# Strassen's identity in the down projection of a linear-attention and feed-forward kernel

## The chip, the cores and the metric

The kernel runs on one core of one Trainium2 chip. A core has five engines that run side by side, each with an instruction queue of its own that it works off in order: TensorE (PE in the profile, with its weight loads as PEld), VectorE (DVE), ScalarE (ACT), GpSimd (POOL) and SyncE (SP), which here only issues DMA transfers. They hand work to each other by semaphores. Matmuls write into PSUM, which has 8 banks of 512 four-byte columns in each of 128 partitions. The metric is device time in microseconds (us); lower is better.

## What is computed

Two stages follow each other. The first is attention with a decaying state over 4 sequences of 768 positions and 8 heads of 64; the second is a feed-forward layer, which takes the attention's output as 3,072 tokens of 512 features:

```python
h = x @ w_in                          # (3072, 512) @ (512, 2048)
g = h * (1.0 / (1.0 + np.exp(-h)))    # SiLU
return (g @ w_out).astype(np.float32) # (3072, 2048) @ (2048, 512)
```

Inputs and the output are float32; the kernel multiplies in bf16 and sums in float32.

## The kernel before, in words

**Groups.** The tokens are handled in 12 groups of 256, numbered g = 0 to 11 in the code (the change's "groups 3 to 12" are g = 2 to 11). A group is two chunks of 128 tokens, 24 chunks in all. The attention of a pair of chunks is a "section" of small 64 by 64 matmuls (`section`, the matmuls at line 540). A section can do three things at once: the outputs of one pair of chunks (tile `op`), and the scores (`sp`) and the states (`kv_ps`) of the next pair. Behind its matmuls it puts on VectorE and ScalarE: the copies of the outputs into `xt` (one half of the features on each engine), then on VectorE two masked score copies `ss` (line 560) and for each state an addition to the running `total` (line 570 or 572) and a cast of it to `kvs`.

**Up projection.** `ffn1_two(g, i)`, i = 0 to 7, does 8 matmuls of 256 columns (line 604) into one PSUM bank with the tag "h", and ScalarE then applies SiLU to the whole bank (line 609) and writes a bf16 tile `g` of 2 by 256 columns. There are two "h" banks, so the unit i+2 can't start before the SiLU of unit i has read its bank.

**Down projection.** `downs(g)` gives 8 units of `ffn2`: for each of the two token halves `mt`, four units of 4 matmuls of 512 columns (line 642), which is 32 matmuls per group. Each half fills one bank of tags "o0" and "o1", which take turns, and VectorE copies it to SBUF (line 648), from where SP stores it: outputs of the first six groups wait in the list `held` until no more input loads are to come, later ones go to `stores` and are issued two units later. The last half of the last group is cut in three (`ffn2_last`, line 662), so that its last copy and store are small.

**Order.** The order of the instructions on each engine is the order of the Python calls; nothing reorders them. In the loop at line 807 a group is: 8 up units, then 8 down units. Before the third down unit (i = 2) come the input scaling on GpSimd (`preps`), transposes by DMA and the loads of later chunks; before the second and the fourth come the casts of `v` on ScalarE (`vcast`); before the seventh (i = 6, line 836) comes the section. So when the next group's up projection starts, two down units lie between it and the section. In g = 3 a second section stands before up unit 7 (line 818), and in g = 2 before down unit 1 (line 822). Sections of g = 3 to 9 compute scores and states too; those before i = 6 of g = 2 and g = 10 only outputs.

**PSUM.** The 8 banks are o0, o1, two "h", three "att" and one "kv". The section borrows the free one of o0 and o1 for one score bank (`other()`), and both "h" banks for its outputs.

**Waits.** Dependences between engines are found by the layer that records the program, from the parts of the tiles that instructions read and write.

## Time and profile before

| | us |
|---|---|
| three runs | 206.22, 205.32, 206.63 |
| median of them | 206.22 |
| span of the profiled execution, first to last instruction | 203.8 |
| TensorE busy in it | 196.6 (96%) |
| VectorE busy | 81.5 (40%) |
| ScalarE busy | 90.0 (44%) |
| GpSimd busy | 53.5 (26%) |

The profiled execution's span is 2.4 us under the median of the runs. Busy TensorE time counts each matmul to its modelled end, so that matmuls overlap in it; how fast they really follow each other is read from the chain of waits, where 64 of them or 24 of them stand as one piece with its length. In the profile's rows "out<-in" are tiles, 128x512 the partitions and elements of the tile written, "x368" a count, and then come the total busy time and the mean of one in ns. The granted clock of TensorE is 1.00 in most of the span; it is 0.99 as a mean.

### The profile page before, as it was taken

The numbers are of one execution on the slowest core, as the hardware profiler recorded it, in microseconds if no ns is written. First come the engines' busy times: TensorE is split into PE (matmuls) and PEld (weight loads), VectorE is DVE, ScalarE is ACT, GpSimd is POOL, SyncE is SP. The second block draws the span as 40 slices with busy tenths as digits, with TensorE's granted clock in tenths as the row PEclk, the third lists the DMA queues.
The fourth block names the chain that finished last, engine by engine and source line by source line (L and its number), as shares of the span: only waits on it lengthen the run. The fifth ranks groups of instructions, "written<-read, shape, count | busy, mean of one in ns | idle before, by whom it ended". The sixth has DMA issues, their size and how long they took to land.

```text
span 203.8 us, 6077 instructions
## 1 busy us (share of the span) xinstructions
PE 196.6 (96%) x2636; PEld 130.5 (64%) x2636; DVE 81.5 (40%) x176; ACT 90.0 (44%) x165; POOL 53.5 (26%) x98
## 2 busy tenths in 40 slices
PE   7689999999999899999999999999999999999994
PEld 2368444557747656856856856856856856856854
DVE  1897357294072085515315415414315415412011
ACT  3864973454704731641641641741741741622610
POOL 5240002657062126434425153440400000000000
PEclk9969999999999999999999999999999999999999
DMA  4999999999679949849789594997997601101102
GB/s 107 336 369 408 400 408 270 279 266 211 148 151 164 239 80 246 194 83 227 162 187 201 116 264 91 226 215 169 269 384 152 245 2 55 53 3 55 51 2 103
DMA packets 95579, 38.67 MB, mean 190 GB/s; under 512 B 80960, under 2 KB 88512, under 8 KB 95552
## 3 DMA queue, kind: packets, MB, share of 16 engines
q1 hardware_dynamic: 91248, 37.24, 70.5%
q10 hardware_dynamic: 4304, 1.05, 3.1%
q8 instruction: 20, 0.33, 0.7%
q14 instruction: 7, 0.06, 0.1%
HBM read 27.27 MB, written 6.29 MB: 165 GB/s over the span
## 4 chain that ended last, share of the span: by engine, by line
PE 64%; DMA 2%; SPq 1%; ACT 1%; issue 0%; POOL 0%; DVE 0%
PE o_ps L642 29%; PE h_ps L604 28%; PE op L540 3%; DMA vf<-in_v_dram 2%; PE o_part L662 2%; PE sp L540 1%; SPq L391 1%; PE kv_ps L540 1%; ACT vb L178 0%; POOL kb L364 0%; ACT g L609 0%; DVE ob L182 0%; SPq L390 0%
## 5 line engine op out<-in xcount | busy, mean ns | idle before, releaser
L642 PE MATMUL o_ps<-w_out_bf,g 128*128 128x512 bf16 x368 | 83.8, 379 | 0.0
L604 PE MATMUL h_ps<-xt,w_in_bf 128*128 128x256 bf16 x672 | 75.7, 273 | 1.0 <-ACT g L609 1.0
L604 PEld LDWEIGHTS <-w_in_bf 128*128 128x128 bf16 x672 | 65.6, 98 | 11.2 <-issue 1.1
L609 ACT ACTIVATE g<-h_ps 128x512 bf16<-128x512 f32 x84 | 49.9, 597 | 41.3 <-PE h_ps L604 41.0
L642 PEld LDWEIGHTS <-g 128*128 128x128 bf16 x368 | 34.8, 98 | 38.3
L178 ACT ACTIVATE xt<-op 128x256 bf16<-128x256 f32 (+1 forms) x18 | 8.3, 487 | 46.9 <-issue 34.4
L364 POOL TENSOR_TENSOR qb<-qf,lam_fwd 128x256 bf16<-128x256 f32 x18 | 11.3, 625 | 59.7 <-issue 31.3
L648 DVE COPY ob<-o_ps 128x512 f32<-128x512 f32 x11 | 7.6, 689 | 46.6 <-PE o_ps L642 46.6
L560 DVE TENSOR_TENSOR ss<-sp,mask 128x512 bf16<-128x512 f32 x20 | 12.8, 682 | 14.9 <-PE sp L540 14.9
L182 DVE CAST xt<-op 128x256 bf16<-128x256 f32 (+1 forms) x16 | 8.3, 543 | 21.2 <-PE op L540 20.1
L648 DVE COPY pair<-o_ps 128x512 f32<-128x512 f32 x12 | 8.2, 686 | 16.5 <-PE o_ps L642 16.5
L572 DVE TENSOR_TENSOR total<-total,kv_ps 128x256 f32<-128x256 f32 x33 | 13.6, 414 | 0.1
L364 POOL TENSOR_TENSOR kb<-kf,lam_bwd 128x256 bf16<-128x256 f32 x20 | 12.4, 618 | 4.6 <-DMA kf<-in_k_dram 3.4
L365 POOL TENSOR_TENSOR kb<-kf,lam_bwd 128x256 bf16<-128x256 f32 x20 | 12.5, 625 | 0.0
L178 ACT ACTIVATE vb<-vf 128x512 bf16<-128x512 f32 x20 | 11.6, 622 | 0.9 <-DMA vf<-in_v_dram 0.9
L365 POOL TENSOR_TENSOR qb<-qf,lam_fwd 128x256 bf16<-128x256 f32 x18 | 11.2, 620 | 0.0
L182 DVE CAST kvs<-total 128x256 bf16<-128x256 f32 x33 | 10.5, 319 | 1.1
L698 PE MATMUL h_ps<-xt,w_in_bf 128*128 128x512 bf16 x48 | 10.5, 379 | 0.0
L540 PEld LDWEIGHTS <-vb 64*64 64x64 bf16 x320 | 7.5, 105 | 4.5 <-issue 4.2
L540 PE MATMUL op<-ss,vb 64*64 64x64 bf16 x320 | 9.9, 199 | 0.0
L540 PE MATMUL op<-qt,kvs 64*64 64x64 bf16 x296 | 9.6, 194 | 0.0
L698 PEld LDWEIGHTS <-w_in_bf 128*128 128x128 bf16 x48 | 4.7, 98 | 5.4
(76 smaller groups left out, 126.2 us busy)
## 6 DMA issues: line engine op xcount, KB each, us to landing
kf<-in_k_dram SPq DMA_DIRECT2D x19, 256.0 KB, 4.5
vf<-in_v_dram SPq DMA_DIRECT2D x18, 256.0 KB, 4.2
qf<-in_q_dram SPq DMA_DIRECT2D x17, 256.0 KB, 4.0
pair<-in_moe_w_out_dram SPq DMA_DIRECT2D x8, 512.0 KB, 7.8
pair<-in_moe_w_in_dram SPq DMA_DIRECT2D x6, 512.0 KB, 7.3
out_dram<-pair SPq DMA_DIRECT2D x12, 256.0 KB, 3.9
out_dram<-ob SPq DMA_DIRECT2D x11, 256.0 KB, 3.8
pair<-in_k_dram SPq DMA_DIRECT2D x4, 256.0 KB, 4.5
```

The lines of the kernel that those rows point to most:

```text
L178: nc.scalar.activation(dst, src, AF.Copy)
L182: nc.vector.tensor_copy(dst, src)
L364: eng.tensor_tensor(dst[:, 0::2], src[:, 0::2, ::-1, :], by[:, 0::2, ::-1, :], op=AL.mult)
L365: eng.tensor_tensor(dst[:, 1::2], src[:, 1::2], by[:, 1::2], op=AL.mult)
L540: ins = nc.tensor.matmul(dst, lhsT=lhsT, rhs=rhs, start=start, stop=True, skip_group_check=True)
L560: nc.vector.tensor_tensor(ss, sp.rearrange("k w p q -> k (w p) q"), mask64[:, None, :].to_broadcast([128, len(scores) * NP, D]), op=AL.mult)
L572: nc.vector.tensor_tensor(total[b], old, place(c, h), op=AL.add)
L604: nc.tensor.matmul(hps[g, i][:, a:a + 256], lhsT=w_in_bf[:, ko, m * 128:(m + 1) * 128], rhs=xt[g][:, ko, :], start=(ko == 0 and u == 0), s ...
L609: nc.scalar.activation(gg.rearrange("p u n -> p (u n)"), hps[g, i], AF.Silu)
L642: nc.tensor.matmul(o, lhsT=gt[g, ko][:, mt * BLK:(mt + 1) * BLK], rhs=w_out_bf[:, ko, :], start=(ko == 0), stop=(ko == KO_OUT - 1))
L648: nc.vector.tensor_copy(ob, o)
L698: nc.tensor.matmul(hps["m", m], lhsT=w_in_bf[:, ko, m * 128:(m + 1) * 128], rhs=xall[0][:, :, ko, :], start=(ko == 0), stop=(ko == KO_IN - 1))
```

## The change

The down projection of g = 2 to 11 is a product of a 256 by 2048 matrix (the group's `g`, stored transposed) with the 2048 by 512 matrix `w_out`. The change cuts both into 2 by 2 blocks of 128 tokens, 1024 inner positions (8 matmuls, `K2`) and 256 output columns (`HALF`), and replaces the eight block products by Strassen's seven. Each product is 8 matmuls of 256 columns, 56 per group. Groups 0 and 1 stay as they were.

What it needs beside the products:

- `weight_sum`: the five sums and differences of blocks of `w_out` that the identity uses, once, in ten VectorE additions of 128x1024 bf16 elements. Four come before g = 2, six between its first up units.
- `g_sums(g, i)`, after each up unit: for i < 4 one VectorE subtraction of 128x256 bf16 elements (`gd`), for i > 3 an addition of 128x256 (`gc`), one of 128x512 (`gb`) and a subtraction of 128x256 (`gd`). Operands and results are bf16 in SBUF.
- Recombination in place of the two copies: `after_4`, `after_6`, `after_2` and `after_7`, with float32 operands in PSUM and SBUF.

```diff
-        for i, unit in enumerate(downs(g)):
+            ups(g, i)                              # ffn1_two, then g_sums
+            if g == 2 and i < 6:
+                weight_sum(*sums[4 + i])
+        for i, unit in enumerate(seven(g)):
...
-            if i == 6:
+            if i == 5:
...
-                section((c, d), cs, steps(*cs) if cs else (), "AD", many[:2] if cs else many, other())
+                section((c, d), cs, steps(*cs) if cs else (), "AD", many[:2] if cs else many)
```

The products and what follows each (`seven`; o[0] and o[1] are the banks o0 and o1, each with two places of 256 columns):

```python
def product(g, n, dst, start):
    tick()
    for k in range(K2):
        if n in (3, 4):
            lhsT = gt[g, k][:, 0:128] if n == 3 else gt[g, K2 + k][:, 128:256]
        else:
            lhsT = gs[g, n, k]
        rhs = w_block(n, k, (0, 0))[:, 0, :] if n == 2 else w_block(n, k, (1, 1))[:, 0, :] if n == 5 else wsum[n, k]
        nc.tensor.matmul(dst, lhsT=lhsT, rhs=rhs, start=(start and k == 0), stop=(k == K2 - 1), skip_group_check=True)
...
def after_4():
    nc.scalar.activation(m, o[0][:, 0, :], AF.Copy)
    nc.vector.tensor_tensor(m, m, o[0][:, 1, :], op=AL.add)
def after_6():
    nc.vector.tensor_tensor(m, m, o[1][:, 0, :], op=AL.add)
def after_2():
    nc.vector.tensor_tensor(quarters[:, 0::3, :], m[:, None, :].to_broadcast([128, 2, HALF]), o[0], op=AL.subtract)
    nc.scalar.activation(quarters[:, 1:3, :], o[0], AF.Copy)
    if last:
        put(0, (HALF, DM), quarters[:, 1, :])
        put(1, (0, HALF), quarters[:, 2, :])
        nc.vector.tensor_tensor(quarters[:, 3, :], quarters[:, 3, :], o[1][:, 1, :], op=AL.add)
        put(1, (HALF, DM), quarters[:, 3, :])
def after_7():
    if last:
        nc.vector.tensor_tensor(quarters[:, 0, :], quarters[:, 0, :], tail, op=AL.add)
        put(0, (0, HALF), quarters[:, 0, :])
        return
    nc.vector.tensor_tensor(quarters[:, 0::3, :], quarters[:, 0::3, :], o[1], op=AL.add)
...
order = [(3, 0, 0, True, None), (4, 0, 1, False, after_4), (1, 1, 0, True, None), (6, 1, 1, False, after_6),
         (5, 0, 0, False, None), (2, 0, 1, False, after_2), (7, 1, 0, True, after_7)]
```

`quarters` is the output tile of the group as four pieces of 256 columns: token half 0 in pieces 0 and 1, token half 1 in pieces 2 and 3. Product 2 and product 5 use blocks of `w_out` as they are, products 3 and 4 blocks of `g` as they are. For the last group product 7 goes to an "h" bank (`tail`), and the four pieces are stored one by one (`put` issues the DMA at once); `ffn2_last` goes away.

In the loop, the section now stands before the sixth of seven products (product 2), and no longer borrows an "o" bank; its third bank comes from "att". The ring of output tiles has 2 tiles of 1,024 columns in place of 4 of 512.

More of the change, by code (lines that the diff above doesn't have):

```diff
@@ L67 @@
     gpool = ctx.enter_context(tc.tile_pool(name="gpool", bufs=26))
-    opool = ctx.enter_context(tc.tile_pool(name="opool", bufs=4))
+    opool = ctx.enter_context(tc.tile_pool(name="opool", bufs=2))
     psum = ctx.enter_context(tc.tile_pool(name="psum", bufs=1, space=bass.MemoryType.PSUM))
@@ L611, in ffn1_close @@
             gt[g, 2 * i + u] = gg[:, u, :]
+        gt[g, 2 * i, "pair"] = gg
     def ffn1_two(g, i):
@@ L646, in ffn2 @@
             nout[0] += 1
-            ob = opool.tile([128, DM], F32, name="ob", tag="ob") if n > 11 else pairs[n // 2][:, DM * (n % 2):DM * (n % 2) + DM]
+            ob = pairs[n // 2][:, DM * (n % 2):DM * (n % 2) + DM]
             nc.vector.tensor_copy(ob, o)
             r0 = gstart[g] + mt * BLK
-            dst = out[r0:r0 + BLK, :]
-            if n > 11:
-                stores.append([0, dst, ob])
-            else:
-                held.append((dst, ob))
-    def ffn2_last(g, mt):
-        r0 = gstart[g] + mt * BLK
-        for i, (a, z, tag) in enumerate([(0, 256, "o"), (256, 384, "h"), (384, 512, "h")]):
-            o = psum.tile([128, 512], F32, name="o_part", **bank(tag))
-            for ko in range(KO_OUT):
-                nc.tensor.matmul(o[:, :z - a], lhsT=gt[g, ko][:, mt * BLK:(mt + 1) * BLK], rhs=w_out_bf[:, ko, a:z],
-                                 start=(ko == 0), stop=(ko == KO_OUT - 1))
-            ob = opool.tile([128, DM], F32, name="ob", tag="ob")
-            move("A" if i == 1 else "D", ob[:, :z - a], o[:, :z - a])
-            tick(0)
-            nc.sync.dma_start(out=out[r0:r0 + BLK, a:z], in_=ob[:, :z - a])
+            held.append((out[r0:r0 + BLK, :], ob))
@@ new lines, with w_block, weight_sum @@
+    HALF = DM // 2
+    K2 = KO_OUT // 2
+    wsum = {}
+    WSUMS = (
+        (3, "subtract", (0, 1), (1, 1), "kp"),
+        (4, "subtract", (1, 0), (0, 0), "vp"),
+        (1, "add", (0, 0), (1, 1), "qtp"),
+        (6, "add", (0, 0), (0, 1), "ktp"),
+        (7, "add", (1, 0), (1, 1), "qb2"),
+    )
+    def w_block(n, k, blk, size=1):
+        row, col = blk
+        return w_out_bf[:, K2 * row + k:K2 * row + k + size, HALF * col:HALF * col + HALF]
+    def weight_sum(i, h):
+        n, op, a, b, tag = WSUMS[i]
+        t = nat.tile([128, K2 // 2, HALF], BF16, name=f"wsum{n}", tag=tag, bufs=2)
+        k = K2 // 2 * h
+        nc.vector.tensor_tensor(t, w_block(n, k, a, K2 // 2), w_block(n, k, b, K2 // 2), op=getattr(AL, op))
+        for x in range(K2 // 2):
+            wsum[n, k + x] = t[:, x, :]
@@ new lines, with g_sums @@
+    gs = {}
+    def g_sums(g, i):
+        lo, hi = slice(0, 128), slice(128, 256)
+        one = gt[g, 2 * i, "pair"]
+        first = i < K2 // 2
+        d = gpool.tile([128, 2, 128], BF16, name="gd", tag="g", padded_shape=[128, 2, 256])
+        if not first:
+            low = gt[g, 2 * i - K2, "pair"]
+            cross = gpool.tile([128, 2, 128], BF16, name="gc", tag="g", padded_shape=[128, 2, 256])
+            nc.vector.tensor_tensor(cross, low[:, :, lo], one[:, :, hi], op=AL.add)
+            both = gpool.tile([128, 2, 256], BF16, name="gb", tag="g")
+            nc.vector.tensor_tensor(both, low, one, op=AL.add)
+        a, b = (hi, lo) if first else (lo, hi)
+        nc.vector.tensor_tensor(d, one[:, :, a], one[:, :, b], op=AL.subtract)
+        for u in range(2):
+            k = 2 * i + u - (0 if first else K2)
+            gs[g, 6 if first else 7, k] = d[:, u, :]
+            if not first:
+                gs[g, 1, k] = cross[:, u, :]
+                gs[g, 5, k] = both[:, u, lo]
+                gs[g, 2, k] = both[:, u, hi]
@@ new lines, in product, with seven, put, step @@
+    def product(g, n, dst, start):
+        tick()
+        for k in range(K2):
+            if n in (3, 4):
+                lhsT = gt[g, k][:, 0:128] if n == 3 else gt[g, K2 + k][:, 128:256]
+            else:
+                lhsT = gs[g, n, k]
+            rhs = w_block(n, k, (0, 0))[:, 0, :] if n == 2 else w_block(n, k, (1, 1))[:, 0, :] if n == 5 else wsum[n, k]
+            nc.tensor.matmul(dst, lhsT=lhsT, rhs=rhs, start=(start and k == 0), stop=(k == K2 - 1), skip_group_check=True)
+    def seven(g):
+        o = [psum.tile([128, 2, HALF], F32, name="o_ps", **bank("o")) for _ in range(2)]
+        last = g == len(GROUPS) - 1
+        tail = psum.tile([128, HALF], F32, name="o_tail", tag="h", bufs=2, padded_shape=[128, 512]) if last else None
+        ob = pairs[g] if g < 6 else opool.tile([128, 4 * HALF], F32, name="ob", tag="ob")
+        quarters = ob.rearrange("p (a n) -> p a n", a=4)
+        m = work.tile([128, HALF], F32, name="msum", tag="msum", bufs=2)
+        r0 = gstart[g]
+        def put(rows, cols, src):
+            dst = out[r0 + BLK * rows:r0 + BLK * rows + BLK, cols[0]:cols[1]]
+            if last:
+                nc.sync.dma_start(out=dst, in_=src)
+            elif g < 6:
+                held.append((dst, src))
+            else:
+                stores.append([0, dst, src])
+        def after_4():
[12 more added lines that the diff above has]
+        def after_7():
+            if last:
+                nc.vector.tensor_tensor(quarters[:, 0, :], quarters[:, 0, :], tail, op=AL.add)
+                put(0, (0, HALF), quarters[:, 0, :])
+                return
+            nc.vector.tensor_tensor(quarters[:, 0::3, :], quarters[:, 0::3, :], o[1], op=AL.add)
+            for t in range(2):
+                put(t, (0, DM), ob[:, DM * t:DM * t + DM])
+        order = [(3, 0, 0, True, None), (4, 0, 1, False, after_4), (1, 1, 0, True, None), (6, 1, 1, False, after_6),
+                 (5, 0, 0, False, None), (2, 0, 1, False, after_2), (7, 1, 0, True, after_7)]
+        def step(n, b, x, start, after):
+            def run():
+                product(g, n, tail if n == 7 and last else o[b][:, x, :], start)
+                if after:
+                    after()
+            return run
+        return [step(*x) for x in order]
@@ L794, with ups @@
     down0(3, 1)
-    def downs(g):
-        return [(g, mt, range(4 * kk, 4 * kk + 4)) for mt in range(2) for kk in range(4)]
-    def other():
-        return f"o{1 - otag[0]}", 1
+    sums = [(i, h) for i in range(len(WSUMS)) for h in range(2)]
+    for x in sums[:4]:
+        weight_sum(*x)
     def steps(*cs):
         return [(c, h) for c, h in [(cs[0] - 1, 1)] + [(c, h) for c in cs for h in range(2)] if c > 5][:-1]
+    def ups(g, i):
+        ffn1_two(g, i)
+        g_sums(g, i)
     many = (("h", 2),) * 2 + (("att", 3),) * 2
@@ L819 @@
                 section((), (c, d), steps(c, d))
-            ffn1_two(g, i)
-        for i, unit in enumerate(downs(g)):
+            ups(g, i)
+            if g == 2 and i < 6:
+                weight_sum(*sums[4 + i])
+        for i, unit in enumerate(seven(g)):
             if i == 1 and g == 2:
                 section((), (c, d), steps(c, d))
-            if i == 1 and g > 2:
+            if i == 2 and g > 2:
                 vcast(a)
@@ L835 @@
                 load_vs(10, 11, e=nc.scalar)
-            if i == 6:
+            if i == 5:
                 cs = [x for x in (a, b) if g > 2 and x < NCHUNK]
-                section((c, d), cs, steps(*cs) if cs else (), "AD", many[:2] if cs else many, other())
-            ffn2(*unit)
+                section((c, d), cs, steps(*cs) if cs else (), "AD", many[:2] if cs else many)
+            unit()
     g = len(GROUPS) - 1
     for i in range(8):
-        ffn1_two(g, i)
-    for unit in downs(g)[:4]:
-        ffn2(*unit)
-    ffn2_last(g, 1)
+        ups(g, i)
+    for unit in seven(g):
+        unit()
 _INS = ['q', 'k', 'v', 'lam', 'moe_w_in', 'moe_w_out']
```

## The prediction, made before the changed kernel ran

> **What bounds the kernel now.** I read the page first: which engine is full, and what the chain that ended last is made of.

> ```profile
> PE 196.6 (96%) x2636; PEld 130.5 (64%) x2636; DVE 81.5 (40%) x176; ACT 90.0 (44%) x165; POOL 53.5 (26%) x98
> ...
> PE o_ps L642 29%; PE h_ps L604 28%; PE op L540 3%; DMA vf<-in_v_dram 2%; PE o_part L662 2%; PE sp L540 1%; SPq L391 1%; PE kv_ps L540 1%; ACT vb L178 0%; POOL kb L364 0%; ACT g L609 0%; DVE ob L182 0%; SPq L390 0%
> ```

> TensorE is the path; VectorE has room as a mean. Next the chain in order of time through one group (g = 7), since busy time counts overlapped matmuls twice (start, length, both us).

> ```profile
> 126.45 6.99 PE h_ps L604 x64
> 133.44 5.18 PE o_ps L642 x24
> 138.62 0.15 PE op L540 x2
> ...
> 140.01 1.83 PE o_ps L642 x8
> ```

> A group is 6.99 us of up projection, 7.01 (5.18 + 1.83) of down projection and a section of about 1.4 between its two parts. 64 matmuls of 256 columns take 6.99, so 0.1092 each; 24 of 512 take 5.18, so 0.2158. Cost per column is nearly the same, weight loads (98 ns each in the page's groups) are hidden at either width.

> Third, the timeline of VectorE and, below it, of ScalarE, behind the section that ends at 93.88:

> ```profile
> 94.10 0.69 DVE L182 CAST xt<-op 128x512 bf16<-128x512 f32 x1 [2.37 <-PE op L540]
> 94.70 1.28 DVE L560 TENSOR_TENSOR ss<-sp,mask 128x512 bf16<-128x512 f32 x2
> ...
> 97.66 0.30 DVE L182 CAST kvs<-total 128x256 bf16<-128x256 f32 x1
> 97.87 0.69 DVE L648 COPY pair<-o_ps 128x512 f32<-128x512 f32 x1
> ```

> ```profile
> 96.70 0.60 ACT L609 ACTIVATE g<-h_ps 128x512 bf16<-128x512 f32 x1 [2.12 <-PE h_ps L604]
> 97.57 0.60 ACT L609 ACTIVATE g<-h_ps 128x512 bf16<-128x512 f32 x1 [0.28 <-PE h_ps L604]
> ```

> VectorE works for nearly 4 us behind a section, past the next up projection's start (95.79 in the chain). The copy of the down result comes last, at 97.87, though its bank was full at 95.79. That is harmless now: nobody waits for it. Meanwhile ScalarE does the first SiLU at 96.70.

> **The change, part by part.**

> *Products.* 56 x 0.1092 = 6.12 us in place of 7.01: -0.89 in nine groups; the last has 3.45 + 3.55 = 7.00, so -0.88. Sum -8.9.

> *The copy in after_2.* This decides. VectorE subtracts into pieces 0 and 3 of the output tile, then ScalarE copies pieces 1 and 2. They are disjoint, but the stretch from piece 0 to piece 3 covers 1 and 2. In the built program the ScalarE copy waits for VectorE at the subtraction's count and not for TensorE. The subtraction stands on VectorE behind the whole section; the copy stands on ScalarE ahead of all SiLUs of the next group; the third up unit needs the first SiLU. From the up projection's start T:

> - The subtraction can start when the copy at L648 starts now: D = 3.25, 2.08, 2.77, 2.74, 2.10, 2.72 and 2.71 after T, for the sections of g = 3 to 9 (97.87 - 95.79 = 2.08 is g = 4; the two short ones have three states, the others four). Two products (1.75) lie behind the section where 1.83 lay, so add 0.08.
> - Subtraction 0.68 (row ss, 682 ns, same size, one operand in PSUM), hand-over 0.05, copy 0.60 (row xt<-op on ACT), of which the next ACT instruction waits 0.50 (starts in a back-to-back pair differ by that), SiLU 0.60, hand-over 0.04.
> - The SiLU ends at T + D + 1.95; the third unit wants to start at T + 1.75. Stall: D + 0.20.

> Sum over seven: 18.37 + 1.4 = 19.8 us. With free hand-overs, and ScalarE's next instruction charged nothing beyond the subtraction: D - 0.39, 15.6. Later SiLUs come every 0.50, units every 0.87, so no second stall. In g = 2 and 10 the section leaves only output copies and the subtraction is in time.

> *Small sums.* No bf16 addition from SBUF is in the trace. Nearest rows: a bf16 to bf16 copy of 512 elements takes 424 ns where f32 to bf16 takes 692, so 16-bit data go at the double rate; at that rate 256, 512 and 1024 elements cost 0.21, 0.34 and 0.61 us back to back (the last by the w_out cast, 693 ns). At the single rate (rows total and ss) 0.33, 0.60 and about 1.2. I take the double rate. Per up unit with i > 3 that is 0.76 against 0.87 of TensorE: VectorE keeps up, and product 1, the first to need `gc`, starts two products later. At the single rate the backlog is four times 0.4, and product 1 has 1.5 us of slack: about nothing.

> *Products 5 and 7* wait for after_4 and after_6. after_4 is 0.42 on ACT and 0.41 on DVE while products 1 and 6 (1.75) run: hidden, if VectorE is free. *ScalarE's after_4 copy* delays the two casts of v by 1.3 us; they still end before the section needs them (0.8 left). *Stores and loads on SP* move with their units; SP waits for after_7, with nothing urgent behind. The third "att" bank is drained a group earlier. All nothing.

> *First group (g = 2).* VectorE is not free here. From 48.4 (its last copy) it does 10 x 0.61 + 12 x 0.21 + 4 x 0.34 = 10.0 us, plus collisions: a cast at 83.16 took 0.73 in place of 0.29 while GpSimd worked, 0.44 per collision. Three such are 1.3: 59.7. Then the scores and states of the section put before product 4 (3.2), and after_4 (0.41): 63.3. Product 5 would start at 54.6 + 4 x 0.874 + 0.65 = 58.8, so 4.5 lost; of it 1.0 returns, since g = 3 now waits 1.0 for ScalarE (longest wait of TensorE on `g`), held by a DMA. Net +3.5. Bounds: no collision +2.2, all eleven GpSimd operations there +7.0, single rate +12. [...]

> *g = 3* has a section before up unit 7: its VectorE work ends 2.69 after the up projection now (74.96 - 72.27), `gc` of unit 7 follows (0.3), product 1 needs it at 2.4: +0.55.

> *End.* Behind product 2: subtraction, ACT copy, three stores on SP, then the last. By rows 0.68 + 0.60 + 4 x 0.40 (three issues in 1.99 now, with waits) against one copy and one issue behind the last matmul: +1.5; 0.5 to 2.

> *Clock.* A gap of 2 to 3 us on TensorE is new. By windows of 3.41 us:

> ```profile
> 8.69:12.10 3.41, 2.27 (x77) 1.80 (x76) 3.41 (x6) 2.64 (x7) 1.82 (x2) 1.00 1.14 343
> 12.10:15.51 3.41, 3.26 (x74) 2.66 (x75) 2.73 (x6) 2.06 (x6) 1.16 (x1) 0.50 1.06 382
> ```

> After a window with PE busy 2.27 of 3.41 (small overlapped matmuls; by columns at 0.427 ns a column I count 45% streaming) the granted clock was 0.50 for one window. A gap of 2.9 that falls mostly within one window leaves about 15 to 40%. Each half-clock window under dense work costs 1.7. Eight gaps: 0 to 13.6. The group's new length, 14.2 + 2.9, is about five windows, so gaps repeat one phase and a half-clock window shifts it: I take two, +3.4.

> [...]

> **Sum.** -8.9 + 19.8 + 3.5 + 0.55 + 1.5 = +16.45 without the clock; span 203.8 to 220.3, time 206.22 to 222.7. With two half-clock windows: 226.

> **Rivals.**

> - *Clock stays full* (none or one half window): 222.7 to 224.4. [...] Against: the row at 12.10.
> - *Every gap halves it* (five to eight): 231 to 236.
> - *Faster:* the copy is released by TensorE at product 2's end, or VectorE gets to the subtraction early. Without the 19.8 and the clock: 202.9. It decides where the mean stall drops under 0.48 us (3.35 / 7), that is where the section's VectorE work ends 0.3 after T, not 2.6. Against: every one of the seven D, and the wait in the program.
> - *VectorE is the bound:* single-rate sums, +8.5 in g = 2: 231 to 235.
> - *Seven products aren't cheaper,* since more weight loads show: at 98 + 109 ns a product matmul, +4.6 a group, far over 240. The 64 matmuls in 6.99 have just as many loads and hide them.

> **How the numbers follow.** Chances: two to four half windows (225 to 230) 0.40; clock full 0.27; every gap 0.13; VectorE bound 0.07; stalls by their lower bound or partly hidden (208 to 219) 0.06; faster 0.04; within 1% 0.03. Range 216 to 236: the low end is 222.7 with stalls (-4.2), g = 2 (-1.3) and end (-1.0) at their lower bounds, the high end the eight-gap case. A difference of 1% is about what a measurement of this kernel can tell. Faster 0.04, within 1% 0.03, slower 0.93.

> **What would show it.** In the changed profile: waits of TensorE (h_ps, L604) for ACT g of 2 to 3.5 us, seven of them in g = 4 to 10, and in each case the ScalarE copy (L741) starting right behind VectorE's L740, itself right behind `kvs`. Products at 0.109 us a matmul. A wait of product 5 for VectorE in g = 2. Granted clock 0.50 behind some gaps. I am wrong if the copy at L741 starts with product 2's end while VectorE is still at `kvs`, if the stalls are there but under 1 us, or if products take over 0.12 us a matmul.

## The result, and the profile after

| | before | after |
|---|---|---|
| median, us (executions) | 206.24 (4) | 234.27 (4: 229.93 to 239.94) |
| profiled execution, us | – | 232.78 |
| its span, us | 203.8 | 231.1 |

The ratio is 1.124, with an interval of 1.114 to 1.135: the change makes the kernel slower by 12%, which is 231.8 us by the ratio. The ratio leaves out executions more than 1.5% above the fastest, two of these four. All sums that follow are made on the profiled execution, whose span grew by 27.3 us.

The page first: the busy times of the engines, and their shares of the chain that ended last:

```profile
PE 198.3 (86%) x2844; PEld 156.0 (68%) x2844; DVE 144.5 (63%) x366; ACT 97.9 (42%) x184; POOL 59.4 (26%) x98
...
PE 64%; DVE 24%; ACT 3%; issue 3%; DMA 2%; SPq 2%; DVEq 0%; ACTq 0%
```

TensorE fell from 96% to 86% of the span, and in the chain that ended last VectorE now holds 24%, where its entry in the line of before rounds to 0%. VectorE as a mean is still at 63%: it isn't full, it is in the way at certain places. TensorE's waits say at which (line waited at, who was waited for, us in total, times, the longest):

```profile
PE h_ps L604 <- ACT g L609: 17.5, 7, 3.0
PE o_ps L711 <- DVE msum L734: 3.1, 2, 2.8
PE o_ps L711 <- DVE gc L689: 2.5, 3, 2.0
```

Before, the first of these was one single wait:

```profile
PE h_ps L604 <- ACT g L609: 1.0, 1, 1.0
```

The seven waits lie in g = 4 to 10, one in each. The chain of waits through one of them, from the section of g = 5 into the up projection of g = 6, in order of time (start, length, both us):

```profile
122.17 0.38 PE op L540 x28
122.55 0.67 DVE xt L182
...
126.94 0.29 DVE kvs L182
127.24 0.61 DVE pair L740
...
127.93 0.07 ACT pair L741
...
128.42 0.60 ACT g L609
...
129.06 7.07 PE h_ps L604 x48
```

After the section's last matmul the path leaves TensorE, runs through all of VectorE's work behind the section, then the subtraction (L740), then the ScalarE copy (L741), then the SiLU, and comes back to TensorE at 129.06. In the timelines, the copy on ScalarE and, below it, TensorE's restart:

```profile
127.93 0.60 ACT L741 ACTIVATE pair<-o_ps 128x512 f32<-128x512 f32 x1 [4.76 <-DVE pair L740]
```

```profile
129.06 1.14 PE L604 MATMUL h_ps<-xt,w_in_bf 128*128 128x256 bf16 x9 [3.01 <-ACT g L609]
```

ScalarE stood for 4.76 us, released by VectorE's L740. Two up units (16 matmuls) ran from 124.15; both "h" banks were then full, ScalarE couldn't read them, and TensorE stood for 3.01 us.

The second thing the page of after shows is in its line of granted clocks (tenths of full speed, 40 slices). The upper line is before, with one dip in the third slice; the lower is after:

```profile
PEclk9969999999999999999999999999999999999999
PEclk9959999999979979799999799799999999999998
```

The time from the start of one group's up projection to the next, in us, places the stalls and the dips. g = 11 runs to the end of the span.

| g | 2 | 3 | 4 | 5 | 6 | 7 | 8 | 9 | 10 | 11 |
|---|---|---|---|---|---|---|---|---|---|---|
| before | 15.74 | 17.18 | 15.23 | 15.18 | 15.48 | 15.39 | 15.19 | 15.20 | 14.80 | 16.91 |
| after | 20.37 | 19.37 | 18.95 | 16.78 | 19.32 | 18.72 | 16.67 | 18.25 | 16.09 | 17.86 |
| of it windows at half clock | 1 | 1 | 1 | 0 | 1 | 1 | 0 | 0 | 0 | 0 |

Groups 4 to 10 grew by 18.3 us together, groups 2 and 3 by 6.8, the last by 0.95, and the first up projection of g = 2 starts 1.2 later, behind a second half-clock window at 11 to 18 us where the profile of before has one (no part of the change lies there). Together 27.3.

### The profile page after: what moved, and what is told of

Read it like the earlier page. It is cut to its first block, busy times and chain, and to the rows that moved or that the text cites. A ratio compares the mean times of both kernels' runs of the same rounds, so it can differ in the third digit from the quotient of the medians.

```text
span 231.1 us, 6726 instructions
## 1 busy us (share of the span) xinstructions
PE 198.3 (86%) x2844; PEld 156.0 (68%) x2844; DVE 144.5 (63%) x366; ACT 97.9 (42%) x184; POOL 59.4 (26%) x98
## 4 chain that ended last, share of the span: by engine, by line
PE 64%; DVE 24%; ACT 3%; issue 3%; DMA 2%; SPq 2%; DVEq 0%; ACTq 0%
PE h_ps L604 25%; PE o_ps L711 20%; PE o_ps L643 6%; PE h_ps L797 4%; DVE ss L560 4%; DVE total L572 4%; DVE kvs L182 4%; PE op L540 3%; DVE wsum L674 3%; ACT g L609 3%; DMA pair<-in_k_dram 2%; SPq L224 2%; DVE xt L182 2%; DVE ob L740 1%; DVE gb L691 1%
## 5 line engine op out<-in xcount | busy, mean ns | idle before, releaser
L604 PE MATMUL h_ps<-xt,w_in_bf 128*128 128x256 bf16 x672 | 81.8, 282 | 17.5 <-ACT g L609 17.5
L604 PEld LDWEIGHTS <-w_in_bf 128*128 128x128 bf16 x672 | 67.6, 101 | 29.9 <-issue 18.7
L609 ACT ACTIVATE g<-h_ps 128x512 bf16<-128x512 f32 x84 | 49.1, 597 | 30.3 <-PE h_ps L604 30.2
L693 DVE TENSOR_TENSOR gd<-g 128x256 bf16<-128x256 bf16 x80 | 25.6, 320 | 22.6 <-ACT g L609 22.5
L364 POOL TENSOR_TENSOR qb<-qf,lam_fwd 128x256 bf16<-128x256 f32 x18 | 15.9, 884 | 62.8 <-issue 36.8
L711 PE MATMUL o_ps<-w_out_bf,gb 128*128 128x256 bf16 x160 | 22.5, 287 | 3.9 <-DVE msum L734 3.1
L711 PE MATMUL o_ps<-wsum,gd 128*128 128x256 bf16 x152 | 20.5, 280 | 0.0
L711 PEld LDWEIGHTS <-gb 128*128 128x128 bf16 x160 | 15.6, 102 | 7.1 <-issue 4.5
L178 ACT ACTIVATE xt<-op 128x256 bf16<-128x256 f32 (+1 forms) x18 | 8.3, 485 | 28.3 <-PE op L540 28.0
L711 PE MATMUL o_ps<-wsum,g 128*128 128x256 bf16 x160 | 19.3, 273 | 0.0
L182 DVE CAST xt<-op 128x256 bf16<-128x256 f32 (+1 forms) x16 | 8.3, 543 | 17.2 <-PE op L540 15.9
L711 PEld LDWEIGHTS <-gd 128*128 128x128 bf16 x160 | 16.1, 101 | 2.2
L691 DVE TENSOR_TENSOR gb<-g 128x512 bf16<-128x512 bf16 x40 | 17.5, 438 | 0.0
L689 DVE TENSOR_TENSOR gc<-g 128x256 bf16<-128x256 bf16 x40 | 12.4, 311 | 7.3 <-ACT g L609 6.5
L711 PEld LDWEIGHTS <-g 128*128 128x128 bf16 x160 | 15.6, 98 | 1.8
L364 POOL TENSOR_TENSOR kb<-kf,lam_bwd 128x256 bf16<-128x256 f32 x20 | 12.8, 641 | 10.2 <-PE kv_ps L540 9.2
L643 PE MATMUL o_ps<-w_out_bf,g 128*128 128x512 bf16 x64 | 14.8, 379 | 0.0
L572 DVE TENSOR_TENSOR total<-total,kv_ps 128x256 f32<-128x256 f32 x33 | 13.6, 414 | 0.1
L741 ACT ACTIVATE ob<-o_ps 128x512 f32<-128x512 f32 x6 | 3.6, 598 | 22.6 <-DVE ob L740 22.6
L711 PE MATMUL o_ps<-wsum,gc 128*128 128x256 bf16 x80 | 10.9, 273 | 2.5 <-DVE gc L689 2.5
L560 DVE TENSOR_TENSOR ss<-sp,mask 128x512 bf16<-128x512 f32 x20 | 12.8, 681 | 0.2 <-PE sp L540 0.2
```

The source lines that it names most:

```text
L182: nc.vector.tensor_copy(dst, src)
L364: eng.tensor_tensor(dst[:, 0::2], src[:, 0::2, ::-1, :], by[:, 0::2, ::-1, :], op=AL.mult)
L560: nc.vector.tensor_tensor(ss, sp.rearrange("k w p q -> k (w p) q"), mask64[:, None, :].to_broadcast([128, len(scores) * NP, D]), op=AL.mult)
L572: nc.vector.tensor_tensor(total[b], old, place(c, h), op=AL.add)
L604: nc.tensor.matmul(hps[g, i][:, a:a + 256], lhsT=w_in_bf[:, ko, m * 128:(m + 1) * 128], rhs=xt[g][:, ko, :], start=(ko == 0 and u == 0), s ...
L609: nc.scalar.activation(gg.rearrange("p u n -> p (u n)"), hps[g, i], AF.Silu)
```

## The experiments

Four kernels were run first, beside the kernel before on one chip (its median there: 205.44). Theory A is the prediction's: the ScalarE copy of pieces 1 and 2 is tied to VectorE's subtraction, VectorE is late behind each section, and ScalarE's queue stands. Theory B: the larger VectorE work, the sums and the recombination, holds TensorE whatever the order. Theory C is about the clock: it falls because TensorE stands in the gaps, so it would not fall if they were filled with other work.

### The ScalarE copy ahead of the subtraction (copy_first)

```diff
 def after_2():
+    if not last:
+        nc.scalar.activation(quarters[:, 1:3, :], o[0], AF.Copy)
     nc.vector.tensor_tensor(quarters[:, 0::3, :], m[:, None, :].to_broadcast([128, 2, HALF]), o[0], op=AL.subtract)
-    nc.scalar.activation(quarters[:, 1:3, :], o[0], AF.Copy)
+    if last:
+        nc.scalar.activation(quarters[:, 1:3, :], o[0], AF.Copy)
```

> The changed kernel with two lines of after_2 swapped in all groups but the last: the ScalarE copy of pieces 1 and 2 is issued ahead of the VectorE subtraction, so it waits for TensorE alone, and the subtraction (which VectorE reaches late anyway) waits for the copy. Theory (the held copy makes the stalls): the seven waits of the up projection for SiLU (17.5 us in the changed profile) vanish, and with them the half-clock windows behind those gaps (three of the five that the change added, 1.7 us each). What stays: products -8.9, first-group waits +5.6 less 1.0, end +1.9, up to two half-clock windows in g = 2 and 3 (+3.4): 204 to 210 us. Rival (VectorE's added load, or dearer products, holds the groups): the up projections still wait for SiLU or the products for sums, over 220 us.

Measured: 210.21 us (209.41 to 212.09, 4 executions), ratio 1.022 (1.016 to 1.028). No instruction was taken away, two changed places, and some 21 us went by the ratios (22.8 by the spans of the profiled executions). The timelines of ScalarE and, below it, of VectorE behind the section of g = 5:

```profile
116.83 0.60 ACT L741 ACTIVATE pair<-o_ps 128x512 f32<-128x512 f32 x1 [0.36 <-PE o_ps L711]
118.52 0.60 ACT L609 ACTIVATE g<-h_ps 128x512 bf16<-128x512 f32 x1 [1.09 <-PE h_ps L604]
```

```profile
120.72 0.68 DVE L742 TENSOR_TENSOR pair<-msum,o_ps 128x512 f32<-128x512 f32 x1
```

Now the copy is released by TensorE (L711), 3.9 us ahead of the subtraction, and the SiLU waits for its own matmuls only. VectorE is as late as ever (120.72), and no unit waits for it. The waits for ACT g are gone from TensorE's list; those of the first groups stay (3.3 us in all for `gc`, 3.2 for `msum`).

Groups 4 to 10 now take 102.3 us together, against 106.5 before and 124.8 after. So A holds and B falls for these groups; what B describes is seen in g = 2 and 3 alone, where copy_first loses 7.9 us against before, two half-clock windows among it.

### The same two instructions in the kernel before (before_wait, before_split)

The second copy of the down result in g = 3 to 9 is cut in two, with the engines and the interleaving of the change (pieces of 128 columns here, of 256 there) but no Strassen product and no block sum:

```diff
-            nc.vector.tensor_copy(ob, o)
+            if mt == 1 and 3 <= g <= 9:
+                ob4, o4 = (t.rearrange("p (a n) -> p a n", a=4) for t in (ob, o))
+                nc.vector.tensor_copy(ob4[:, 0::3, :], o4[:, 0::3, :])
+                nc.scalar.activation(ob4[:, 1:3, :], o4[:, 1:3, :], AF.Copy)
+            else:
+                nc.vector.tensor_copy(ob, o)
```

That is before_wait. before_split has the ScalarE line above the VectorE line.

> The kernel before, with its 512-column products, but the copy of the second token half of g = 3 to 9 cut in two in the way of after_2: VectorE copies pieces 0 and 3, then ScalarE copies pieces 1 and 2 of 128 columns each, and so waits for VectorE. Theory (the wait alone costs it): each of the seven next up projections stalls by D - 0.3 us (copies of 256 elements instead of 512), 16 us in all, plus nothing to seven half-clock windows: 222 to 232 us. Rival (the cost lies in Strassen's sums or products): within 1% of 206 us.

> As the run with the wait alone, with the same instructions in the other order: the ScalarE copy of pieces 1 and 2 first, then VectorE's copy of pieces 0 and 3. Theory: ScalarE copies at once, is done before the first SiLU, nothing stalls: 206 us, within 1%. Rival (a copy on ScalarE delays the SiLUs whatever it waits for): several us over 206.

Measured: before_wait 226.59 us (226.49 to 227.89, 4), ratio 1.102 (1.097 to 1.107); before_split 205.26 us (204.31 to 207.01, 10), ratio 0.999 (0.996 to 1.003). ScalarE's copy in before_wait, and TensorE's wait:

```profile
120.21 0.38 ACT L651 ACTIVATE pair<-o_ps 128x256 f32<-128x256 f32 x1 [4.24 <-DVE pair L650]
```

```profile
PE h_ps L604 <- ACT g L609: 16.3, 8, 2.8
```

And in before_split, the same copy:

```profile
110.55 0.38 ACT L650 ACTIVATE pair<-o_ps 128x256 f32<-128x256 f32 x1 [1.11 <-PE o_ps L642]
```

TensorE's wait for ACT g is 0.7 us there, once. The two kernels differ in the order of two instructions that touch no common element, and by 10%. VectorE writes pieces 0 and 3, ScalarE pieces 1 and 2 between them. When ScalarE is second it waits 4.24 us for VectorE, with the next group's SiLUs behind it. When VectorE is second, ScalarE is long done. The stall needs neither Strassen's products nor its sums. In before_wait, too, three half-clock windows follow the gaps (mean granted clock 0.976 in the profiled execution); they and the stalls make groups 4 to 10 21.8 us longer than before.

Why the layer that records the program ties the two is another question, and the prediction's reason (the stretch from piece 0 to piece 3 covers pieces 1 and 2) doesn't fit the trace. In the changed kernel the addition of after_7 (L753) writes pieces 0 and 3 of the same tile and is issued behind the ScalarE copy, yet it doesn't wait for it. In the stretch shown in the result the copy runs from 127.93 to 128.53, and VectorE has

```profile
127.94 0.69 DVE L753 TENSOR_TENSOR pair<-pair,o_ps 128x512 f32<-128x512 f32 x1
```

The two run side by side like this in g = 3 to 10. What the subtraction and the copy share, and L753 does not, is the PSUM bank that they read: both read o[0], L753 reads o[1]. The two copies of before_wait and before_split read one bank as well. So the bank read by both engines is the likely tie; no run here tests it, for instance by the same pieces read from two banks.

### The gaps filled with matmuls of zeros (gap_filled)

The changed kernel with 8 matmuls of 512 columns on zeros before the third up unit of g = 4 to 10, where TensorE stands. They add work that the output doesn't use:

```diff
 def ups(g, i):
+    if g in range(4, 11) and i == 2:
+        fill(psum.tile([128, 512], F32, name="warm_ps", **bank("att")), 16)
     ffn1_two(g, i)
```

> The changed kernel with eight zero matmuls of 512 columns (1.7 us) put into a free bank before up unit 2 of g = 4 to 10, that is into each of the seven gaps; no result depends on them. Theory (gaps halve the clock): the SiLU waits shrink by 1.7 us each as the zeros fill them, the ends of the gaps don't move, and no half-clock window follows one of the seven gaps; the time falls by about 1.7 us per half-clock window saved, 3 to 5 of them, to 226 to 230 us, and its spread over runs narrows. Rival (the windows come from elsewhere, by chance or by the changed products): as many half-clock windows as before, 234 us or more.

Measured: 227.77 us (226.95 to 229.86, 4), ratio 1.108 (1.101 to 1.115). TensorE's timeline in g = 5:

```profile
105.18 1.91 PE L604 MATMUL h_ps<-xt,w_in_bf 128*128 128x256 bf16 x16
106.93 1.89 PE L206 MATMUL warm_ps<-zero 128*128 128x512 bf16 x8
```

The third up unit comes no earlier than it did (its stalls, counted from the start of the up projection, add up to 19.3 us, against 18.6), now with zeros in the gap, and the clock line of the page has no dip in g = 4 to 10; the one in the middle lies in g = 2:

```profile
PEclk9999999999859999999999999999999999999998
```

Groups 4 to 10 take 120.2 us instead of 124.8: with the three half-clock windows 4.5 us went, so 1.5 each. Theory C holds for these 4.5 us. The four executions lie within 2.9 us of each other, where the four of the changed kernel lie within 10.0. Of those the shortest has the highest mean granted clock (0.976) and the longest the lowest (0.928), but the two between don't follow (232.78 us with 0.945, 235.76 with 0.956). So the spread narrowed when the gaps were filled, and how much of it is half-clock windows stays open.

### Where the seven products pay (from_4, middle)

These two were run together on another chip (median of before there: 206.07). Both have copy_first's order. from_4 takes the identity for g = 4 to 11 alone: g = 2 and 3 use the plain down projection, the ten weight sums stay in g = 2, and the block sums of `g` begin with g = 4. middle leaves the last group plain too, with its three-part end as before.

```diff
+PLAIN = (2, 3)            # middle: (2, 3, 11)
...
-        g_sums(g, i)
+        if g not in PLAIN:
+            g_sums(g, i)
...
-        for i, unit in enumerate(seven(g)):
+        for i, unit in enumerate(downs(g) if g in PLAIN else seven(g)):
```

> The run with the copy issued first (210.2 us), with Strassen's products from g = 4 on only: g = 2 and 3 keep the 32 matmuls of 512 columns, no small sums and the section's old place; the ten sums of weight blocks stay where they are, in g = 2. Theory (in g = 2 and 3 the weight sums and small sums queue on VectorE ahead of the sections' scores, and products 1 and 5 wait): the periods of g = 2 and 3 fall back from 21.3 and 19.5 us to those of the kernel before, 15.7 and 17.2, and nothing else moves: 202 us. Rival (the two groups are slow for another reason, the weight sums themselves or the loads): they stay 3 us or more longer than before, 206 us or more.

> The same, and the last group too keeps its 32 matmuls of 512 columns and its end in three pieces: Strassen in g = 4 to 10 only. Theory (the end of the change costs 1.9 us behind the last matmul and its products save 0.9): 1 us less than the run with Strassen to the end, 201 us, that is the kernel before less seven times 0.6 us, the mean gain of a group in the run with the copy issued first. Rival (the end is hidden behind the stores): 1 us more than that run.

Measured: from_4 202.04 us (201.5 to 202.81, 6), ratio 0.980 (0.977 to 0.983); middle 200.89 us (200.5 to 201.8, 6), ratio 0.975 (0.972 to 0.978). Both are faster than the kernel before and than copy_first. TensorE's chain through g = 4 of middle:

```profile
80.04 7.02 PE h_ps L604 x64
87.06 4.37 PE o_ps L730 x40
...
92.65 1.85 PE o_ps L730 x16
```

It stays on TensorE: 4.37 + 1.85 = 6.22 us for 56 matmuls (seven products), where before had 7.01 for 32 wider ones. In neither kernel does TensorE wait for `gc` or `msum`. What each group gave, in us:

| | g = 2 | 3 | 4 to 10 | 11 |
|---|---|---|---|---|
| before | 15.74 | 17.18 | 106.47 | 16.91 |
| copy_first | 21.34 | 19.47 | 102.34 | 17.83 |
| from_4 | 15.74 | 17.10 | 102.13 | 17.83 |
| middle | 15.74 | 16.15 | 102.18 | 16.97 |

Seven groups give 4.3 us together, 0.61 each (from 0.43 in g = 5 to 0.76 in g = 4). With the weight sums still in it, g = 2 of from_4 is as short as before: those ten additions alone cost nothing there. The last group is dearer by 0.9 with the identity than without. The 0.95 between from_4 and middle in g = 3 is no effect of the edit that I can name: it is the single wait for ACT g that before and from_4 have (1.0 and 0.9 us) and the profile of middle has not.

## Why the prediction was right, and where a term was off

The forecast was 226 us in a range of 216 to 236; the ratio puts the kernel at 231.8, and the median of four is 234.27. Direction, place and the wait that makes the stalls were right. The term for the clock was too small, and the reason given for the wait isn't borne out. The time lies inside the range, but above the band that was called likeliest (225 to 230): the upper end had been set by eight half-clock windows behind gaps, and the time got there with three of those, two in g = 2 and 3, and one more than before at start-up, which is luck.

- **Products: -8.9 forecast.** The rate held: 6.22 us for 56 is 0.111 each, and weight loads (98 to 102 ns each on the page of after) don't show. The gain in the down projection is 0.79 a group rather than 0.89, in the chain because the two products behind the section take 1.85 and not 1.75. Of it 0.61 reached the group's length in middle. The rival "seven products aren't cheaper" is out.
- **The copy in after_2: 19.8 forecast.** This was the decisive step, and that the held copy makes the stalls is shown by copy_first and by the pair in the kernel before. What ties the copy to the subtraction is not the interleaving of the pieces, as L753 shows (in the section on before_wait); the wait itself had been read from the built program, so the sum didn't depend on the reason. Counted as forecast, from T + 1.75 to the third unit's start, the stalls of g = 4 to 10 are 2.92, 2.33, 3.17, 3.01, 2.27, 2.90 and 2.01, together 18.6; the view of waits, which counts idle time alone, has 17.5. The formula D + 0.20 gave 3.45, 2.28, 2.97, 2.94, 2.30, 2.92 and 2.91. Five of seven agree within 0.2. The first was too long because its D came from a row with a collided cast (0.73). In the last, TensorE lost 0.72 us for no reason that the profile shows between the section of g = 9 and the products behind it, so T itself came later and the stall was shorter by about as much. With the products, 19.8 - 6.2 = 13.6 was forecast for g = 4 to 10 at full clock; gap_filled, which has no half-clock window there, grew by 13.8.
- **Small sums: double rate taken.** It held. In g = 2, three additions that follow each other without a hold are

```profile
56.13 0.28 DVE L689 TENSOR_TENSOR gc<-g 128x256 bf16<-128x256 bf16 x1
56.34 0.41 DVE L691 TENSOR_TENSOR gb<-g 128x512 bf16<-128x512 bf16 x1
56.67 0.28 DVE L693 TENSOR_TENSOR gd<-g 128x256 bf16<-128x256 bf16 x1
```

  and what follows each starts 0.21, 0.33 and 0.20 behind it, against 0.21 and 0.34 forecast for 256 and 512 elements; a weight sum of 1024 elements takes 0.60 in the chain, against 0.61. VectorE keeps up from g = 4 on, and the rival "VectorE is the bound" is out.
- **First groups: +3.5 in g = 2 and +0.55 in g = 3.** The mechanism was right (the chain of g = 2 runs through `wsum`, `gd`, `gb`, the section's work and `msum`, and product 5 waits 2.8). Less a half-clock window of 1.7 each, g = 2 grew by 2.9 and g = 3 by 0.5. By the forecast's terms, products taken off, it would have been 4.5 - 0.9 = 3.6 and 0.55 - 1.0 - 0.9 = -1.35: together 2.3, where 3.4 was measured. g = 2 came out cheaper; in g = 3 the wait in product 1 for `gc` is 2.0 us where 0.55 was forecast. Two things make most of the difference. The VectorE work of the section before up unit 7 ends 3.7 us after the up projection and not 2.69, because its first score copy starts at 76.96, behind the sums of units 5 and 6, which the forecast had not put ahead of it: +1.0. Then `gc` itself takes 0.62 in the chain and not 0.3, because it meets GpSimd's work (last section), which had been priced for g = 2 only: +0.3.
- **End: +1.5.** The last group grew by 0.95; with the 0.88 that its products should have saved that is +1.8, within the 0.5 to 2. TensorE's last matmuls and the four last stores are

```profile
225.49 1.04 PE L711 MATMUL o_tail<-wsum,gd 128*128 128x256 bf16 x8
```

```profile
227.04 1.81 SPq L726 DMA_DIRECT2D out_dram<-ob  x4
```

  and SP issues the stores one behind the other, 1.81 us in all, the whole of it behind TensorE's last matmul.
- **Clock: two half windows, +3.4.** This is the mis-sized term. The profiled execution has five in g = 2 to 7, two behind the stalls of the first groups and three behind the new gaps: 8.5 at the forecast's 1.7 each, somewhat less in truth, since the three in g = 4 to 10 cost 4.5 by gap_filled. One more at start-up, 1.2 in the span, isn't of the change. The step that failed is "gaps repeat one phase and a half-clock window shifts it: I take two"; nor had it been asked what the stalls in g = 2 and 3 do to the clock. The rival "every gap halves it" (231 to 236) has the right size but not the right account: three of seven gaps did. The 45% streaming that the prediction counts in the row at 8.69 hangs on the small 64-row matmuls, several of which run at once (16 of 128 columns take 0.42 us there, from 9.40, where 16 times 128 columns at 0.427 ns would be 0.87): by columns they bring the window to 34% if each counts a quarter and to 96% if it counts in full, so no threshold follows from that row.

Summed: start 1.2, g = 2 and 3 without the clock 3.4, g = 4 to 10 without the clock 13.2, the end 0.95, five windows 8.5: 27.25 of 27.3. The sum closes because the terms without the clock were got by taking 1.7 a window off; only the 13.2 has a measurement of its own beside it, the 13.8 of gap_filled.

## What to carry to other kernels

Before moving part of a copy to another engine, look at the instruction it is tied to: two instructions on two engines that read one PSUM bank were ordered here although they write no common element (the second stood for 4.76 us), and the engine that is late had to be issued second. One swapped pair was worth some 21 us of 232. Price an identity that saves matmuls by the engine that pays for it in each stage: the same seven products won 0.6 us a group in the middle, lost 3.4 us in the changed kernel and 4.5 in copy_first in the two groups where VectorE was already busy (two half-clock windows of 1.7 taken off), and lost 0.9 at the end, where nothing hides the recombination. A stall on TensorE is to be charged twice, for its length and for the clock behind it; the second charge came behind three of seven gaps here, some 1.5 us each.

## What the runs showed of the hardware

```profile
89.42:92.83 3.41, 0.90 (x9) 0.66 (x7) 3.08 (x8) 0.88 (x2) 0.00 (x0) 1.00 0.59 134
92.83:96.24 3.41, 3.16 (x16) 2.17 (x16) 1.17 (x3) 1.29 (x3) 2.38 (x4) 0.50 1.16 263
181.57:184.98 3.41, 1.48 (x14) 1.32 (x14) 2.04 (x5) 1.92 (x4) 0.00 (x0) 1.00 0.20 74
184.98:188.39 3.41, 3.41 (x33) 2.97 (x32) 1.93 (x7) 2.30 (x5) 0.00 (x0) 1.00 0.42 162
```

The gap of g = 4 (2.76 us idle) lies almost whole in one window, TensorE is busy 0.90 of 3.41 in it, and the next window is granted 0.50: 16 matmuls, where a window at full clock holds 33; the one after it is at 1.00 again. The gap of g = 9 is 2.74 us long, but begins in the window before; 1.48 us of work are left in this one and the clock stays. In the profiled execution of after, behind the first 25 us, the full-clock windows of this grid with TensorE busy for 0.61, 0.90, 1.30, 1.35 and 1.43 us were each followed by half clock, and none with 1.70 or more was. Between, it went both ways: 1.60 fell, while 1.48 and 1.56 stayed. In the first 25 us, with many small matmuls, it fell behind 2.27 in before (the row in the prediction) and behind 2.37 in after, so busy time alone doesn't sort these windows. A gap of 2 to 3 us cost some 1.5 more here (4.5 for three, by gap_filled) or nothing, and the gaps of g = 4 and g = 9, of 2.76 and 2.74 us, differ by where they lay on the grid.

**VectorE's additions and GpSimd's multiplications wait for each other.** In g = 3 of the changed kernel, timelines of VectorE and GpSimd:

```profile
80.78 0.70 DVE L689 TENSOR_TENSOR gc<-g 128x256 bf16<-128x256 bf16 x1
81.41 0.83 DVE L691 TENSOR_TENSOR gb<-g 128x512 bf16<-128x512 bf16 x1
82.17 0.70 DVE L693 TENSOR_TENSOR gd<-g 128x256 bf16<-128x256 bf16 x1
```

```profile
81.30 0.66 POOL L364 TENSOR_TENSOR kb<-kf,lam_bwd 128x256 bf16<-128x256 f32 x1
81.92 0.79 POOL L365 TENSOR_TENSOR kb<-kf,lam_bwd 128x256 bf16<-128x256 f32 x1
```

Against the rows of g = 2 above, each of the three takes 0.42 us more, whether it has 256 or 512 columns: the two engines' instructions end by turns (VectorE's at 81.48, 82.24 and 82.87, GpSimd's at 81.96 and 82.71). That is near the 0.44 that the prediction took from a cast. In g = 2 GpSimd was the one that stood: its multiplication (L364) at 56.19 took 4.66 us, where the next one, at 60.81, took 0.61; VectorE's sums ran one behind the other meanwhile, until 60.37. What the prediction missed is where it strikes: the first of these additions holds product 1 of g = 3.
